# Seven products in place of eight for seven blocks, another cut of the tokens into blocks, and a written order of all operations

## The chip, the cores and the metric

One core of a Trainium2 chip runs the whole program. The metric is the device time of one execution in microseconds. TensorE (PE) multiplies, VectorE (DVE), ScalarE (ACT) and GpSimd (POOL) do the elementwise work, and SyncE (SP) issues most of the DMAs. Each engine runs its own instructions strictly in the order in which the program lists them, and waits at an instruction whose inputs are not there yet.

## The reference

Attention for 8 batches of 8 heads, 576 positions and 64 columns, twice (pooled by four, and in a band of seven positions), the sum of both, and then two dense layers:

```
q_d, k_d, v_d = mean of q, k, v over groups of 4 positions        # 144 groups
out_d     = softmax(q_d k_d^T / 8) v_d                            # repeated 4 times along the positions
out_local = softmax(q k^T / 8 where |i - j| < 4) v
x   = (out_up + out_local), as 4608 tokens x 512
h   = x @ w_in                                                    # 512 x 2048
out = (h - tanh(h)) @ w_out                                       # 2048 x 512
```

## The kernel before

**Attention.** Work goes by pairs of heads, p = 0 to 31, four pairs to a batch b. For each pair SP issues loads of k and q (`st`, two of 256 KB, `load_qk`) and of v in five overlapping tiles of 128 rows (`vst`, two of 160 KB, `load_v`). The 64 rows that are left of a batch's k and q come in two loads of their own (`sr`, `load_rest`). The casts to bf16 (`qr`, `vw`, `rr`) run on DVE, ACT or POOL. q and k are turned by PE for pairs 0 to 11 (`KIN`) and by a DMA for the others. PE makes the scores (`score1`, `score2`, matmuls with 64 contraction rows), ACT their exponentials (`E`), DVE multiplies by the band's mask, PE sums over v (`outs`, 18 matmuls), DVE divides (`ln`), and the result is turned back and added (`join`) into `xT`, a ring of three batches.

**Pooled v.** `vp` has 144 rows of group sums in two halves: groups 0 to 127, and groups 128 to 143 in the first 16 partitions of the second. For pairs 0 to 11 (`VIN`) PE makes it from `vw` with six matmuls against 0/1 matrices (`pool_v`, `pick`). For pairs 12 to 31 two loads bring v a third time (`load_v4`, 128 and 16 partitions, into buffers that were zeroed once), and two adds on POOL sum it (`pool_v4`, lines 440 and 444).

**Dense layers.** A block is a batch. The 576 columns of a batch in `xT` stand in the order (plane c, group g): column 144 c + g is position 4 g + c. A block kb takes the first 512 columns, and the last 64 of two batches share one more step (`left1`, `left2`). First layer: `mm1`, 16 steps of four 128x512 matmuls, then tanh on ACT (`u`, line 814) and the difference on DVE (`gT`, line 817). Second layer, blocks 0 to 4: `mm2`, 64 matmuls of 128x512 (line 883), four copies out of PSUM and 7 stores. Second layer, blocks 5 to 7 (`SEVEN`): a 2x2 cut of `gT` and `w_out` and seven products in place of eight, after Winograd. Each is 16 matmuls of 128x256 (`product`, line 1030). Its price elsewhere: `token_sums` (line 965) forms four sums of quarters of `gT`, in place for three of them; `weight_sums` (line 939) forms four differences of quarters of `w_out` once; and the results are added up through `keep0` and `y` (lines 1055 and 1101). The matmuls of the second layer of block kb - 1 are given to the planner among those of the first layer of block kb.

**Order.** Every operation is given to a `Plan` with an engine, a duration in ns, what it reads and writes, the PSUM banks that it may take and a priority (`pri`), sometimes an earliest time. `Plan.order` then puts them in order by playing them through on these durations, with a model of the DMA queue; where several engines could take an operation, a string `GIVEN` names the engine or leaves it open. Priority 5000 of the dense matmuls lets everything else go first. `emit` issues the instructions in this order; before the first matmul of block 1 it also puts matmuls on a zeroed tile into gaps (`filler`, line 1240). First-layer outputs and `mm2` outputs share PSUM banks 4 to 7 (`DENSE`), attention has banks 0 to 3.

**Start.** The first queue of w_in loads waits on POOL for the k load of pair 2 (`GATE`) and that of w_out for a v load (`OGATE`).

Of the kernel before, what the change touches and what calls it, by code (L numbers as in the profile page):

```python
# [14 lines left out]
class Plan:  # L15

    LAT = {"PE": 270, "ACT": 160, "DVE": 130, "POOL": 160, "SP": 50, "DMA": 1900,
           "DW": 1900}

    def __init__(self, given):
        self.ops = []
        self.given, self.choices = given, 0
        self.last_write = {}
        self.readers = {}
        self.users = {}  # L30
        self.place = {}

    def op(self, eng, ns, fn, reads=(), writes=(), pri=0, after=0.0, slack=0.0,
           port=False, opens=None, uses=(), choice=None, rows=128, share=0.4):
# [15 lines left out]
        names = set(uses)  # L50
        if opens and not isinstance(opens, list):
            opens = [opens]
        for o in opens or ():
            names.add(o[0])
        for n in names:
            self.users.setdefault(n, []).append(i)
        if choice:

            letter = self.given[self.choices]
            self.choices += 1  # L60
            named = [a[:4] for a in choice if a[0][0] == letter]
            choice = named or [a for a in choice if len(a) == 4]
        alts = {a[0]: a for a in choice} if choice else {eng: (eng, ns, fn, port)}
        self.ops.append(dict(alts=alts, deps=deps, pri=pri, after=after, slack=slack,
                             opens=opens, names=names, rows=rows, share=share,
                             what=(list(writes) + [None])[0]))
        return i

    def order(self):
        ops, n = self.ops, len(self.ops)  # L70
        users = [[] for _ in range(n)]
        left = [0] * n
        for i, o in enumerate(ops):
            left[i] = len(o["deps"])
            for d in o["deps"]:
                users[d].append(i)
        at = [o["after"] for o in ops]
        free, ready = dict.fromkeys(("PE", "ACT", "DVE", "POOL", "SP", "DMA"), 800.0), {}
        start, engine = [None] * n, [None] * n
        pending = {k: len(v) for k, v in self.users.items()}  # L80
        ends = {}
        bank_free = [0.0] * 8
        held = [None] * 8
        port_free = 0.0
        rows = 128
        self.held = []

        def make_ready(i):
            for eng in ops[i]["alts"]:
                ready.setdefault(eng, []).append(i)  # L90

        def seats(i):
            t, got, used = 0.0, [], set()
            for _, cs in ops[i]["opens"] or ():
                best = (float("inf"), None)
                for c in cs:
                    if any(held[b] is not None or b in used for b in c):
                        continue
                    best = min(best, (max(bank_free[b] for b in c), c), key=lambda x: x[0])
                if best[1] is None:  # L100
                    return float("inf"), None
                t = max(t, best[0])
                got.append(best[1])
                used.update(best[1])
            return t, got
        for i in range(n):
            if left[i] == 0:
                make_ready(i)
        for _ in range(n):
            best = None  # L110
            for eng, cand in ready.items():
                if not cand:
                    continue
                fr = free.get(eng, 0.0)
                if eng in ("DMA", "DW"):
                    i = min(cand, key=lambda i: (at[i], i))
                    now = max(fr, at[i])
                else:
                    now, i = None, None
                    eff = []  # L120
                    for c in cand:
                        t = max(at[c], seats(c)[0], fr)
                        if ops[c]["alts"][eng][3]:
                            t = max(t, port_free)
                        eff.append((t, c))
                    now = min(eff)[0]
                    if now == float("inf"):
                        continue
                    i = min((ops[c]["pri"], c) for t, c in eff if t <= now)[1]
                if best is None or now < best[0]:  # L130
                    best = (now, eng, i)
            if best is None:
                raise RuntimeError(f"no operation can be put next: {[(e, [(ops[c].get('what'), at[c], ops[c]['opens']) for c in cs[:6]]) for e, cs in ready.items()]} {held}")
            now, eng, i = best
            for other in ops[i]["alts"]:
                ready[other].remove(i)
            o = ops[i]
            _, ns, fn, port = o["alts"][eng]
            o["fn"], o["ns"] = fn, ns
            for (name, _), c in zip(o["opens"] or (), seats(i)[1] if o["opens"] else ()):  # L140
                self.place[name] = c
                for b in c:
                    held[b] = name
                self.held.append([name, c, now, None])
            start[i], engine[i] = now, eng
            if eng == "PE":

                if o["rows"] != rows:
                    ns += 60 if rows == 128 else 95
                rows = o["rows"]  # L150
            if eng == "DMA":

                ns *= 0.89 if now > 60000 else 0.82

                slow = max(0.0, free.get("DW", 0.0) - now)
                f = o["share"]
                ns = ns / f if ns <= f * slow else ns + (1 - f) * slow
            end = now + ns
            free[eng] = end
            if port:  # L160
                port_free = end
            for name in o["names"]:
                ends[name] = max(ends.get(name, 0.0), end + self.LAT[eng])
                pending[name] -= 1
                if pending[name] == 0:
                    for b in self.place[name]:
                        held[b] = None
                        bank_free[b] = ends[name]
                    for h in self.held:
                        if h[0] == name:  # L170
                            h[3] = ends[name]
            for u in users[i]:
                same = eng in ops[u]["alts"] and len(ops[u]["alts"]) == 1 and \
                    eng not in ("DMA", "DW")
                at[u] = max(at[u], end if same else end + self.LAT[eng] + ops[u]["slack"])
                left[u] -= 1
                if left[u] == 0:
                    make_ready(u)
        self.start, self.engine = start, engine
        return sorted(range(n), key=lambda i: (start[i], i))  # L180

    def emit(self, until=None, filler=None):
        order = self.order()
        stop = min([h[2] for h in self.held if h[0] == until], default=0.0)
        last = 600.0
        for i in order:
            o = self.ops[i]
            if filler and self.engine[i] == "PE" and self.start[i] <= stop:
                gap = self.start[i] - last
                if gap > 350:  # L190
                    busy = {b for _, c, s, e in self.held for b in c
                            if s < self.start[i] and e > last - 300}
                    rest = [b for b in range(7, -1, -1) if b not in busy]
                    if rest:
                        slow = 430 if self.start[i] < 6000 else 230
                        filler(rest[0], int(0.75 * gap / slow))
                last = self.start[i] + o["ns"]
            if o["fn"] is not None:
                o["fn"]()
# [3 lines left out]
def kernel(  # L203
# [48 lines left out]
           170.5, 170.5, 15, 153.5, 207.5, 209.5, 232.5, 235,  # L252
    ]

    GIVEN = (
        "..A..D.DADA.PADDADPDD.AADD..D.DD.AA.DA.ADAA....ADAD..AA..P...AP.D..AP....DDPPPDD"
        "..D..A.A...PAAAPPPAADDD.DDDDAD.ADAD.A..PPPDDDAA...A.....DA..A.AA.PD.D..ADPDDAP.P"
        "D.PP..D.DDDDD.P..DP...DADP...P....A...D.PP..DPAAPP..P.D..AD..A..DD.PPD.PA..D.P.."
# [213 lines left out]
    def attention(p):  # L472
# [248 lines left out]
        def outs():  # L721
            po = at(oname)
            for hh in range(2):
# [6 lines left out]
                for i in range(2):  # L730
                    to(1, EP + 256 * i + 128, vp[s][:, hh, i, :], False, i == 1)
# [540 lines left out]
```

## Time and profile before

| | us |
|---|---|
| median of three runs | 323.43 (322.58 to 326.46) |
| profiled execution, first to last instruction | 320.7 |
| DVE busy, all blocks | 255.3 |
| `L803` first layer, 512 matmuls, busy time | 124.6 |
| `L883` second layer of blocks 0 to 4, 320 matmuls | 78.6 |
| `L1030` seven products of blocks 5 to 7, in three groups by operand (144, 144, 48) | 18.3 + 17.8 + 6.1 |
| `L965` sums of quarters on DVE, blocks 5 to 7 | 6.4 + 4.3 + 4.2 |
| `L440`, `L444` adds of pooled v on POOL, 20 each | 25.4 and 14.6 |
| bytes moved by DMA | 59.23 MB |

A matmul's duration in the trace runs from its issue to a modelled end and overlaps the next one, so a group's mean (379 ns for 128x512) isn't what it costs in a row of matmuls. The cost is the distance from one start to the next, which the chain of waits gives: a piece of it is a stretch of one line's matmuls with start, length and count.

### The profile page before, as it was taken

What the parts mean: (1) busy time and instruction counts of PE and PEld (TensorE: products, weight loads), DVE (VectorE), ACT (ScalarE), POOL (GpSimd) and SP (SyncE); (2) the same over time, 40 slices, a digit from 0 to 9 for tenths busy, and PEclk for the clock granted to TensorE, in tenths of its full rate; (3) what the DMA queues carried; (4) which work ended last, traced back from release to release, by engine and by line L of the source; (5) the groups of instructions that cost most, each with busy time, mean ns of one, the idle gap of its engine ahead of it and who ended that gap; (6) DMA issues with size and microseconds to landing.
All of it is one profiled execution on the core that took longest, in us unless ns stands there. A gap on an engine that the chain in (4) does not pass through costs nothing.

```text
span 320.7 us, 7553 instructions
## 1 busy us (share of the span) xinstructions
PE 309.1 (96%) x2831; PEld 181.0 (56%) x2831; DVE 255.3 (80%) x451; ACT 207.8 (65%) x372; POOL 156.8 (49%) x185
## 2 busy tenths in 40 slices
PE   7978999999999999999999999999899999999994
PEld 3654546554754545454655444545476667666783
DVE  5685997597888898679888999899999797656853
ACT  5884995588856776369745878579766852455210
POOL 7822664326267473537464735357794653511000
PEclk9999999999999999999999999999999999999999
DMA  8999999999999999999999999995452143200414
GB/s 218 275 219 227 279 185 247 289 277 304 240 232 274 236 210 246 224 255 195 245 222 177 269 237 251 232 223 112 94 92 57 35 49 93 67 0 3 130 36 131
DMA packets 117205, 59.23 MB, mean 185 GB/s; under 512 B 85008, under 2 KB 112592, under 8 KB 117168
## 3 DMA queue, kind: packets, MB, share of 16 engines
q1 hardware_dynamic: 111584, 52.17, 71.3%
q0 software_dynamic: 4896, 5.97, 10.0%
q10 hardware_dynamic: 688, 0.61, 0.6%
q8 instruction: 22, 0.36, 0.4%
q14 instruction: 15, 0.12, 0.1%
HBM read 43.65 MB, written 9.44 MB: 166 GB/s over the span
## 4 chain that ended last, share of the span: by engine, by line
PE 88%; DMA 7%; DVE 1%; SPq 1%; ACT 0%; POOL 0%; ACTq 0%; issue 0%; POOLq 0%
PE ps L803 34%; PE ps L883 22%; PE ps L1030 11%; DMA vst<-in_v_dram 6%; PE ps L725 5%; PE ps L829 5%; PE ps L855 4%; PE ps L657 3%; DMA sr<-in_q_dram 1%; PE ps L671 1%; PE ps L510 1%; PE ps L458 1%; PE ps L767 1%; PE ps L665 1%; SPq L366 1%; DVE xT L760 1%
## 5 line engine op out<-in xcount | busy, mean ns | idle before, releaser
L803 PE MATMUL ps<-xT,w_in_sb 128*128 128x512 bf16 x512 | 124.6, 379 | 0.0
L817 DVE TENSOR_TENSOR gT<-ps,u 128x512 bf16<-128x512 f32 x128 | 86.0, 684 | 21.2 <-ACT u L814 19.6
L814 ACT ACTIVATE u<-ps 128x512 f32<-128x512 f32 x128 | 76.1, 599 | 36.2 <-PE ps L803 33.6
L883 PE MATMUL ps<-w_out_sb,gT 128*128 128x512 bf16 x320 | 78.6, 379 | 0.0
L803 PEld LDWEIGHTS <-w_in_sb 128*128 128x128 bf16 x512 | 47.1, 98 | 47.3 <-issue 0.4
L883 PEld LDWEIGHTS <-gT 128*128 128x128 bf16 x320 | 29.2, 98 | 31.2
L444 POOL TENSOR_TENSOR vp<-v 128x256 bf16<-128x256 f32 x20 | 14.6, 730 | 58.7 <-PE ps L725 48.1
L676 ACT ACTIVATE E<-ps 128x912 bf16<-128x912 f32 x32 | 29.8, 931 | 17.8 <-PE ps L665 14.6
L1030 PEld LDWEIGHTS <-gT 128*128 128x128 bf16 x288 | 27.9, 98 | 7.5
L742 DVE TENSOR_TENSOR ln<-ps,r 128x768 bf16<-128x768 f32 x32 | 30.6, 956 | 0.9
L711 DVE TENSOR_TENSOR E<-E,mask 128x1152 bf16<-128x1152 bf16 x29 | 25.6, 882 | 4.4 <-ACT E L680 4.2
L502 POOL CAST qr<-st 128x512 bf16<-128x512 f32 x32 | 22.5, 713 | 9.3 <-DMA st<-in_q_dram 6.0
L440 POOL TENSOR_TENSOR v<-v 128x512 f32<-128x512 f32 x20 | 25.4, 1271 | 1.1
L725 PEld LDWEIGHTS <-E 128*128 128x128 bf16 x576 | 21.7, 97 | 6.1
L684 ACT ACTIVATE E<-ps 128x576 bf16<-128x576 f32 x32 | 20.9, 654 | 0.0
L583 ACT COPY kt<-kq 128x576 bf16<-128x576 bf16 x16 | 18.9, 1180 | 2.9 <-DVE kq L578 2.7
L593 POOL TENSOR_TENSOR half<-kq 128x576 f32<-128x576 bf16 x13 | 18.1, 1389 | 3.6 <-DVE kq L578 1.5
L725 PE MATMUL ps<-vw,E 128*128 128x65 bf16 x320 | 18.9, 193 | 0.0
L760 DVE TENSOR_TENSOR xT<-lT 128x336 bf16<-128x336 bf16 (+1 forms) x30 | 18.4, 655 | 0.0
L1030 PE MATMUL ps<-Tw,gT 128*128 128x256 bf16 x144 | 18.3, 273 | 0.0
L725 PE MATMUL ps<-vp,E 128*128 128x65 bf16 x256 | 18.1, 193 | 0.0
L1030 PE MATMUL ps<-w_out_sb,gT 128*128 128x256 bf16 x144 | 17.8, 273 | 0.0
(118 smaller groups left out, 434.9 us busy)
## 6 DMA issues: line engine op xcount, KB each, us to landing
vst<-in_v_dram SPq DMA_DIRECT2D x64, 160.0 KB, 4.8
st<-in_k_dram SPq DMA_DIRECT2D x32, 256.0 KB, 4.6
st<-in_q_dram SPq DMA_DIRECT2D x32, 256.0 KB, 4.6
v<-in_v_dram SPq DMA_DIRECT2D x14, 256.0 KB, 3.6
w_in_sb<-in_moe_w_in_dram POOLq DMA_DIRECT2D x4, 512.0 KB, 12.7
w_out_sb<-in_moe_w_out_dram POOLq DMA_DIRECT2D x4, 512.0 KB, 12.2
out_dram<-y SPq DMA_DIRECT2D x7, 256.0 KB, 3.8
out_dram<-y SPq DMA_DIRECT2D x7, 224.0 KB, 3.1
```

What stands on the lines that cost most here:

```text
L440: eng.tensor_tensor(out=v2, in0=v4[s][:, :, :, 0:128], in1=v4[s][:, :, :, 128:256], op=ALU.add)
L502: (eng, ns, lambda dst=dst, src=src, fn=fn: fn(out=dst, in_=src), port)
L676: A.activation(out=E[s][:, :, E0:E0 + 456], in_=at(s1)[:, :, PS0:512], func=AF.Exp, scale=SCALE)
L711: eng.tensor_tensor(out=el, in0=el, in1=mask.unsqueeze(1).to_broadcast([128, 2, S]), op=ALU.mult)
L725: T.matmul(po[:, hh, 65 * n:65 * n + 65], E[s][:, hh, e:e + 128], vv, start=start, stop=stop)
L742: op("DVE", 960, lambda: V.tensor_tensor(out=ln[s].rearrange("p n (h d) -> p h n d", d=D), in0=blocks()[:, :, :, 0:64], in1=r[s].unsqueeze ...
L760: eng.tensor_tensor(out=dst, in0=src, in1=add, op=ALU.add)
L803: T.matmul(at(name)[:, 0, :], w_in_sb[:, dc, fc * 128:(fc + 1) * 128], xT[dc][:, c0:c0 + 512], start=(dc == 0), stop=(dc == N_DC - 1))
L814: op("ACT", 600, lambda: A.activation(out=u[us], in_=at(name)[:, 0, :], func=AF.Tanh), reads=[("hd", kb, fc)], writes=[("u", us)], pri=-1, ...
L817: op("DVE", 690, lambda: V.tensor_tensor(out=gT[g][:, fc, :], in0=at(name)[:, 0, :], in1=u[us], op=ALU.subtract), reads=[("hd", kb, fc), ( ...
L883: T.matmul(at(name)[:, 0, :], gT[g][:, fc, ts * 128:ts * 128 + 128], w_out_sb[:, fc, :], start=(fc == 0), stop=(fc == N_FF - 1))
L1030: T.matmul(dst, left[:, f, 128 * j:128 * j + 128], right[:, f, :], start=(first and e == 0 and f == 0 and (j == 0 or apart)), stop=(e == 1 ...
```

## The change

- `SEVEN` is `01111111`: blocks 1 to 4 also make seven products. `weight_sums` then comes with block 1; its earliest time of 180 us is gone.
- A block is made of groups 0 to 127 of all four planes: `mm1` reads `xT` as four runs of 128 columns. The last 16 groups of all planes, positions 512 to 575 of the batch, are the shared step. A pair of planes is then stored by one DMA (two runs of 2 KB per partition); 63 stores of `y` become 20.
- Pooled v: `vp` keeps groups 0 to 127 alone. The 16 groups that are left come for all 8 heads of a batch in one load (`load_vr`, 128 KB) and are summed and spread by three operations per batch on DVE or POOL (`pool_vr`) into `vpr`, which is zero outside a head's 16 partitions. `score2` takes the last groups' scores from a window that is shifted per head, so that they meet these partitions. `pool_v` has five matmuls, `load_v4` one DMA, and the adds of `pool_v4` are half as wide; they may go to DVE. The zeroing of `vp` and of the v4 buffers is gone.
- `Plan` no longer works out an order. Strings name it (`TURNS`), the engine of each choice (`ENGINES`), the banks (`BANKS`) and the filler matmuls (`FILL`, 22 of them; 19 before). The dependencies are checked; the durations in the calls are no longer used.
- The table of ACT's function is loaded by a copy of one element at the start.

```
-    SEVEN = [c == "1" for c in "00000111"]
+    SEVEN = [c == "1" for c in "01111111"]
...
-            for n, (i, t) in enumerate(((0, 0), (0, 1), (0, 2), (0, 3), (0, 4), (1, 4))):
-                T.matmul(pv[:, i, :], pick[:, n, :], vw[w][:, :, t, 0:D],
-                         start=n in (0, 5), stop=n in (4, 5))
+            for t in range(NT):
+                T.matmul(at(name)[:, 0, 0:2 * D], pick[:, t, :], vw[w][:, :, t, 0:D],
+                         start=t == 0, stop=t == NT - 1)
...
+    def load_vr(b):
+        base = v[b, 0]
+        load(500, lambda: nc.sync.dma_start(out=vr[b % 2], in_=bass.AP(
+            tensor=base.tensor, offset=base.offset + 512 * D,
+            ap=[[S * D, H], [4 * D, 16], [1, 4 * D]])),
+            [("vr", b % 2)], 520, 40 * b - 3000 + 4)
...
+        def spread(eng):
+            eng.tensor_tensor(out=vpr[b % 2], in0=vrp.unsqueeze(1).to_broadcast([128, H, D + 1]),
+                              in1=hsel.unsqueeze(2).to_broadcast([128, H, D + 1]), op=ALU.mult)
...
+        w0 = [128 - 16 * (2 * j + hh) for hh in range(2)]
...
-                             qkd[s][rows, 128 * i:128 * i + 128],
+                             qkd[s][rows, w0[hh] * i:w0[hh] * i + 128],
...
+                pools = vp[s][:, hh, :], vpr[b % 2][:, 2 * j + hh, :]
                 for i in range(2):
-                    to(1, EP + 256 * i + 128, vp[s][:, hh, i, :], False, i == 1)
+                    to(1, EP + 256 * i + 128, pools[i], False, i == 1)
...
-                         xT[dc][:, c0:c0 + 512], start=(dc == 0), stop=(dc == N_DC - 1))
+                         xT[dc][:, c0:c0 + S].rearrange("p (c g) -> p c g", c=4)[:, :, 0:128],
+                         start=(dc == 0), stop=(dc == N_DC - 1))
...
+            row = out[kb * S + 4 * r0 + 2 * half + js[0]]
+            (nc.sync if queue == "SP" else nc.scalar).dma_start(
+                out=bass.AP(tensor=row.tensor, offset=row.offset + lo,
+                            ap=[[4 * Dm, n], [Dm, len(js)], [1, hi - lo]]),
+                in_=y[ys][r0:r1, js[0]:js[-1] + 1, lo:hi])
...
+    def emit(self, filler):
+        turn = [self.number(self.turns[2 * i:2 * i + 2]) for i in range(n)]
...
+        for i in turn:
+            fn, deps, opens, names = self.ops[i]
+            assert deps <= done, "an operation stands before what it needs"
```

## The prediction

> **What bounds the kernel now.** First the head of the page and its slices.
>
> ```profile
> span 320.7 us, 7553 instructions
> PE 309.1 (96%) x2831; PEld 181.0 (56%) x2831; DVE 255.3 (80%) x451; ACT 207.8 (65%) x372; POOL 156.8 (49%) x185
> PE   7978999999999999999999999999899999999994
> DVE  5685997597888898679888999899999797656853
> PEclk9999999999999999999999999999999999999999
> DMA  8999999999999999999999999995452143200414
> PE 88%; DMA 7%; DVE 1%; SPq 1%; ACT 0%; POOL 0%; ACTq 0%; issue 0%; POOLq 0%
> ```
>
> PE is full from the fourth slice to the last but one at an undisturbed clock, and it is 88% of the chain of waits (last line); DMA's 7% lies in the first 30 us. DMA, too, is full, but only until slice 27 (some 216 us). Since "busy" PE can hide slow matmuls, I read the chain's pieces (start, us, what) for the cost of one matmul and for the idle moments.
>
> ```profile
> 29.60 0.73 POOL vw L427
> 30.38 0.51 PE ps L458 x6
> 62.50 0.45 PE ps L458 x6
> 127.24 5.61 PE ps L883 x26
> 144.65 5.18 PE ps L803 x24
> 230.18 1.08 DVE E L711
> 295.02 1.79 PE ps L829 x32
> 304.24 12.24 PE ps L1030 x112
> ```
>
> 128x512 costs 0.216 us (5.61/26, 5.18/24), a product's 128x256 costs 0.109 (12.24/112), a step of the shared tokens 0.056 (1.79/32), a `pick` matmul 0.075 at most (0.45/6). From 30.38, where the wait for `vw` of pair 4 ends, PE waits once: about 1.1 us around 231, behind the mask multiply on DVE. It ends at 304.24 + 12.24 = 316.48; last add and store take the other 4.2.
>
> All matmuls of the program at these prices (attention's by the starts in the trace) are 291.1 us, 14.9 of them before 30.38. So 276.2 us of matmuls take 286.1. Of the 9.9 left over 1.1 is the wait, and 8.1 lies where PE goes from full matmuls to score matmuls of 64 rows and back: by the starts in the trace 0.096 on the way in, 0.12 on the way out, 0.02 between the groups, 37 times. Nothing else is lost: what PE no longer does, the kernel no longer takes, as long as the others keep up.
>
> **The products.** In blocks 1 to 4, 256 matmuls at 0.216 (55.3 us) become 448 at 0.109 (48.8): -6.5 us, all on the path. The rows that bear on a risk of it are the weight loads:
>
> ```profile
> L829 PEld LDWEIGHTS <-w_in_sb 128*128 128x128 bf16 x256 | 15.1, 98 | 3.2 <-issue 1.3
> L1030 PEld LDWEIGHTS <-gT 128*128 128x128 bf16 x288 | 27.9, 98 | 7.5
> ```
>
> 98 ns for a weight load of the full array. The change adds 192 loads; exposed, they would cost 18.8 us. The rows exclude it: a step of 0.056 with a load of 0.098 for each matmul is only possible if loads overlap matmuls, and 0.109 would be 0.207. The Trainium skill (TensorE: Matmul & The Clock Gate, the section on packing small matmuls) says that a weight load overlaps running matmuls only when its row group differs; all these loads take the whole array, so by it this change would lose. The trace disagrees, so it stays a rival with a small chance.
>
> **Pooled v.** Twelve pairs with five `pick` matmuls for six: 12 x 0.06 to 0.075, -0.8 us. Operand runs of 128 columns in `mm1` and of 16 in the shared step: no row shows the latter; `L657` reads runs of 28 in 215 ns a matmul, as `L665` does runs of 30 in 216, so I take nothing, with +14 us (a doubled 0.056 for 256 steps) as the far end, held unlikely by these rows.
>
> **Order on PE.** By the program's listing, score groups are entered 31 times after the first dense run, not 37: 6 x 0.22, -1.2 us with the few steps between groups. The wait at 231 is not in a written order by itself: -1.1, or 0 if it returns.
>
> **The start.** PE can run dense once batch 0's `xT` and the first w_in chunk are there. Before:
>
> ```profile
> 13.33 3.17 POOL L408 DMA_DIRECT2D w_in_sb<-in_moe_w_in_dram  x4
> 14.33 1.03 SPq L390 DMA_DIRECT2D vst<-in_v_dram  x2
> 20.54 6.72 SPq L390 DMA_DIRECT2D vst<-in_v_dram  x2
> ```
>
> The four w_in DMAs land at 22.3, 25.7, 29.0 and 33.1 by the trace's landings, and while they run SP's own loads crawl: `vst` of pair 4, issued at 14.85, lands at 29.45, and PE waits for it until 30.38. In the new listing POOL issues the first two w_in chunks only behind both casts of pair 4, whose q is the 19th load on SP. SP's first 16 loads land 0.84 us apart from 3.70 on, and three of the 19 are half loads: about 18.2. A cast of 0.7, issue at 18.9; the first chunk then lands 8.9 later as before, 27.8, the second 3.4 after it. The v of pairs 0 to 3 comes before that (about 20.5 for the last, pair 2's), and cast, pick, sums, division, turn and join follow in some 5 us, so `xT` is there first. On PE two matmuls and a score group lead; the long run starts at 28.5 with 13.9 us of work behind it, where before it was 30.38 with 14.9: -0.9. Ends: -3.5, if the chunk comes at 25, limited by `xT`; +4, if it takes the 12.7 us that the page gives as w_in's median. The third and fourth chunk follow eight and four POOL operations later and land by this reckoning at 35 to 41, a few us ahead of their matmuls; w_out, if issued at 40 (38.2 before), lands from 47 to 60 by the spacing of before (4.2), and the listing takes block 0's second layer quarter by quarter of w_out between 49 and 59: tight, a us late at the end.
>
> **Cover by the other engines.** DVE, by each operation's mean: sums of quarters 5.4 us and adds 2.1 per block, four blocks, so +30; the weight differences (8 x 0.78) only move forward. The strings take away copies of `y`, `kt` and `keep` (9.8), joins (9.2), pooled sums of q and k (7.4), casts and others (5): by the rows -1, and with 29 new small operations, whose nearest row is a copy of 256 columns (`L463`, 0.42; I take 0.3), +8 of 277. POOL: 40 us of `L440` and `L444` shrink to about 15, joins, `qkd` and casts come in. ACT +3 to 7. None is on the path if DVE holds.
>
> ```profile
> 30.00:300.00 270.00, 268.65 (x2382) 152.53 (x2382) 224.57 (x373) 185.06 (x328) 139.98 (x156) 1.00 0.83 186
> 180.00:220.00 40.00, 40.00 (x320) 19.72 (x319) 37.16 (x63) 29.48 (x50) 19.86 (x23) 1.00 0.97 228
> ```
>
> (us, PE, PEld, DVE, ACT, POOL, clock, DMA.) DVE is at 83% between 30 and 300 and was held at 93% for 40 us with PE full. Its 225 us become about 233 in 260: 90%. The DMA's transfers come to the same sum (`vr` +1 MB, the 16-partition loads -0.6, fewer stores); batch 3's last input lands at 99 before, and block 3 now starts some 13 us earlier, at about 126: cover remains.
>
> New waits have no row. I take +1.5 us (the last w_out chunk, or one wait like that at 231), from 0 to 7, one of 1 us for each of seven blocks.
>
> **Sum.** -6.5 - 0.8 - 1.2 - 1.1 - 0.9 + 1.5 = -9.0: span 311.7. The median lies 2.7 above this span, so 323.4 - 9.0 = 314.4.
>
> **Rivals.** (a) *The gain is mostly given back in waits*: start +4 in place of -0.9, new waits 7 in place of 1.5: 314.4 + 10.4 = 324.8; half of that, 319.6, is its likely form. For: the start's chunks are just in time. Against: one wait of 1.1 us in 286 shows how well these streams can be packed. Chance 0.22, within 2%. (b) *DVE takes over in blocks 1 to 4, slower*: sums of quarters read all of a block's `gT` in place, so a late DVE holds `gT`, the four banks that `mm1` writes into fill, and PE stands. It decides where DVE, as the pacer, is busy for less than 83%: 233/0.83 = 281 us between start and tail in place of 260, +18 to 20, time 333. Behind a late sum there wait `gT` (128 x 0.684), and ACT's tanh for its buffers.
>
> ```profile
> DVE gT L817 <- ACT u L814: 19.6, 39, 2.7
> ```
>
> This idle time of DVE is of that sort, it waits for ACT. Against: 93% between 180 and 220. Chance 0.05. (c) *Weight loads exposed*, at every product of blocks 1 to 4: -9.0 + 18.8, time 333; it decides from the first product on. Chance 0.03. This is what the rule of the Trainium skill named above would do here. (d) *More is gained*: start -3.5, no new waits: 310.3. Same verdict as the forecast. That seven products are made at all is settled by the listing: 784 matmuls on the line of the products, 64 on that of `mm2`.
>
> **Numbers.** Forecast with (d) 0.70, (a) 0.22, (b) and (c) 0.08. The range goes from (d), 310, to the middle of (a), 320.5, which leaves some 0.1 above and less below. Two per cent, 317.0 and 329.9, is about what runs between 322.6 and 326.5 can tell from no change. A forecast from 310 to 317 is faster by over 2%; (a) lies within; (b) and (c) are slower.
>
> **What would show it.** Right: in the chain pieces of the products' line at 0.109 a matmul in blocks 1 to 4; a last matmul near 307.5; `L803`'s successor starting its long run at 27 to 30; PE's waits together under 3 us after it. Wrong: a chain with DVE or `gT` in it for some us per block (b); product steps above 0.15 (c); the shared step above 0.056; PE waiting for w_in or w_out between 28 and 58 (a).

## The result and the profile after

The changed kernel takes 371.9 us (median of four runs, 371.1 to 376.9) where the kernel before takes 324.1 (one run more than in the table above): the ratio, taken without the slowest run of the changed kernel, is 1.146 with a 95% interval of 1.139 to 1.152. The forecast was 314.4 us and the range ended at 320.5. The profiled execution has a span of 369.4 us instead of 320.7.

The head of the page of after, its row of granted clock and its chain by line:

```profile
span 369.4 us, 7865 instructions
...
PE 355.5 (96%) x3014; PEld 219.7 (59%) x3014; DVE 265.5 (72%) x463; ACT 211.0 (57%) x380; POOL 173.8 (47%) x221
...
PEclk9999999999699999999589999998589999996599
...
PE ps L782 26%; PE ps L1003 20%; PE ps L809 15%; PE ps L835 5%; DMA vst<-in_v_dram 4%; PE ps L863 4%; PE ps L705 3%; DMA w_in_sb<-in_moe_w_in_dram 3%; DVE gT L938 2%; DMA st<-in_q_dram 2%; PE ps L635 2%; DMA sr<-in_k_dram 1%; DVE gT L797 1%; DVE S L938 1%; PE ps L651 1%
```

PE is as full as before, 96%, so the engines do not starve it: it is busy for 46 us longer (355.5 against 309.1). The third biggest line of the chain is L809, the first layer of the shared step (`left1`, L829 before), 15% of 369 us. And the granted clock, 9 in every slice before, falls to 5 or 6 in four places. Pieces of the chain (start, us, what) give the price of a step:

```profile
84.38 3.56 PE ps L809 x16
88.98 7.14 PE ps L809 x32
...
118.86 2.59 PE ps L782 x12
...
155.34 1.75 PE ps L1003 x16
...
353.27 11.80 PE ps L1003 x108
```

A step of the shared tokens costs 0.223 us (3.56/16, 7.14/32), four times the 0.056 of before. A product in block 2 (155) and in block 7 (353) costs 0.109, `mm1` 0.216, as forecast. The group of L809 shows it as well, once one knows that its mean of 400 ns per matmul contains the overlap with the next:

```profile
L809 PE MATMUL ps<-xT,w_in_sb 128*128 128x128 bf16 x256 | 58.3, 400 | 0.0
L809 PEld LDWEIGHTS <-w_in_sb 128*128 128x128 bf16 x256 | 30.3, 118 | 26.9 <-issue 0.6
```

58.3 us of busy time for 256 matmuls, with an idle time of 0.0 before them: nothing is waited for, the matmul itself is slow. In the windows below (us, then busy time and count of PE, PEld, DVE, ACT, POOL, the granted clock, DMA share, GB/s) the second and fourth hold passes of the shared step:

```profile
110.00:168.00 58.00, 56.95 (x565) 38.42 (x564) 55.89 (x87) 44.69 (x77) 39.53 (x44) 1.00 1.02 225
168.00:192.00 24.00, 24.00 (x126) 13.06 (x125) 13.42 (x23) 7.98 (x14) 6.23 (x11) 0.72 0.63 129
192.00:248.00 56.00, 54.94 (x498) 35.98 (x497) 46.64 (x73) 40.39 (x69) 33.65 (x37) 1.00 0.88 192
...
328.00:352.00 24.00, 24.00 (x98) 11.77 (x97) 11.25 (x16) 6.54 (x12) 0.00 (x0) 0.64 0.06 23
```

Until the last matmul the clock falls only where the shared step runs, to 0.72 and 0.64 on average in these windows. By the trace's records it is at 0.5 for 6.83, 13.65, 13.65 and 17.07 us, beginning 3.4 to 8.2 us after the pass does. The first time is at 92.43, so the sixteen steps from 84.38 on took their 0.223 us while the clock was still at 1.00: the clock isn't what makes the step slow.

I added up all distances between the starts of neighbouring matmuls from 31 us to the last one, and split them by the prices above. `runs16_keep` is an experiment further down, the changed kernel with two repairs. Full price is what each matmul costs in an undisturbed row.

| from 31 us on, against before | forecast | after | `runs16_keep` |
|---|---|---|---|
| all matmuls at full price (275.5 before) | -7.3 | -6.5 | -6.7 |
| changes to and from score matmuls (8.1) | -1.2 | -1.1 | -0.8 |
| waits of PE (1.3) | +0.4 | +5.1 | +7.5 |
| shared step above 0.056 (0.2) | 0 | +42.6 | -0.1 |
| other matmuls while the clock is at 0.5 | 0 | +8.4 | 0 |
| sum | -8.1 | +48.5 | -0.1 |

The forecast's ninth microsecond, -0.9 for an earlier start, lies before 31 us. PE had done 19.4 us of matmuls by then in after and 19.5 before, but that counts the filler matmuls, which compute nothing: 22 of 0.216 us in after, 18 before. Without them it is 14.6 against 15.6, so the start came out about 0.9 us worse instead of better. The same 0.9 explains the first row: over the whole program the matmuls other than fillers fall by some 7.4 us, as forecast, but more of them lie behind 31 us.

### The profile page after: what moved, and what is told of

Its sections match the earlier page's. It is cut to its first block, busy times and chain, and to the rows that moved or that the text cites. A ratio compares the mean times of both kernels' runs of the same rounds, so it can differ in the third digit from the quotient of the medians.

```text
span 369.4 us, 7865 instructions
## 1 busy us (share of the span) xinstructions
PE 355.5 (96%) x3014; PEld 219.7 (59%) x3014; DVE 265.5 (72%) x463; ACT 211.0 (57%) x380; POOL 173.8 (47%) x221
## 4 chain that ended last, share of the span: by engine, by line
PE 78%; DMA 10%; DVE 8%; issue 2%; ACT 1%; ACTq 0%; SPq 0%; POOL 0%; DVEq 0%; POOLq 0%
PE ps L782 26%; PE ps L1003 20%; PE ps L809 15%; PE ps L835 5%; DMA vst<-in_v_dram 4%; PE ps L863 4%; PE ps L705 3%; DMA w_in_sb<-in_moe_w_in_dram 3%; DVE gT L938 2%; DMA st<-in_q_dram 2%; PE ps L635 2%; DMA sr<-in_k_dram 1%; DVE gT L797 1%; DVE S L938 1%; PE ps L651 1%
## 5 line engine op out<-in xcount | busy, mean ns | idle before, releaser
L794 ACT ACTIVATE u<-ps 128x512 f32<-128x512 f32 x128 | 73.6, 599 | 38.6 <-PE ps L782 35.0
L1003 PEld LDWEIGHTS <-gT 128*128 128x128 bf16 x672 | 65.6, 100 | 20.5 <-issue 3.4
L782 PEld LDWEIGHTS <-w_in_sb 128*128 128x128 bf16 x512 | 48.0, 98 | 48.5 <-issue 1.4
L809 PE MATMUL ps<-xT,w_in_sb 128*128 128x128 bf16 x256 | 58.3, 400 | 0.0
L809 PEld LDWEIGHTS <-w_in_sb 128*128 128x128 bf16 x256 | 30.3, 118 | 26.9 <-issue 0.6
L1003 PE MATMUL ps<-w_out_sb,gT 128*128 128x256 bf16 x336 | 45.9, 283 | 0.5 <-DVE y L1027 0.5
L577 POOL TENSOR_TENSOR qkd<-half 128x288 bf16<-128x288 f32 x25 | 23.9, 957 | 45.2 <-DVE half L572 28.0
L1003 PE MATMUL ps<-Tw,gT 128*128 128x256 bf16 x336 | 42.3, 273 | 2.7 <-DVE gT L938 1.5
L822 DVE TENSOR_TENSOR gL<-ps,u 128x512 bf16<-128x512 f32 x16 | 11.1, 691 | 41.8 <-ACT u L820 41.8
L484 POOL CAST qr<-st 128x512 bf16<-128x512 f32 x40 | 27.1, 685 | 29.4 <-DMA kq<-qr 14.6
L820 ACT ACTIVATE u<-ps 128x512 f32<-128x512 f32 x16 | 9.6, 597 | 46.8 <-PE ps L809 46.8
L1074 POOL TENSOR_TENSOR y<-y,keep 128x512 f32<-128x512 f32 x12 | 17.0, 1414 | 16.2 <-ACT y L1024 16.2
L1024 ACT COPY y<-ps 128x512 f32<-128x512 f32 x19 | 11.1, 586 | 21.0 <-PE ps L1003 19.2
```

The costliest lines, as they stand in the source:

```text
L484: (eng, ns, lambda dst=dst, src=src, fn=fn: fn(out=dst, in_=src), port)
L577: eng.tensor_tensor(out=pooled, in0=half[:, 0:288].rearrange("p (n x) -> p n x", n=2), in1=half[:, 288:576].rearrange("p (n x) -> p n x", ...
L782: T.matmul(at(name)[:, 0, :], w_in_sb[:, dc, fc * 128:(fc + 1) * 128], xT[dc][:, c0:c0 + S].rearrange("p (c g) -> p c g", c=4)[:, :, 0:128 ...
L794: op("ACT", 600, lambda: A.activation(out=u[us], in_=at(name)[:, 0, :], func=AF.Tanh), reads=[("hd", kb, fc)], writes=[("u", us)], uses=[n ...
L809: T.matmul(at(name)[:, 0, 128 * f:128 * f + 128], w_in_sb[:, dc, (f0 + f) * 128:(f0 + f) * 128 + 128], xT[dc].rearrange("p (b c g) -> p b ...
L1003: T.matmul(dst, left[:, f, 128 * j:128 * j + 128], right[:, f, :], start=(first and e == 0 and f == 0 and (j == 0 or apart)), stop=(e == 1 ...
```

## The experiments

**Why the shared step is slow.** The line of the diff that I misread is the operand's last one:

```
xT[dc].rearrange("p (b c g) -> p b g c", b=NR, c=4)[:, s0:s0 + 2, 128:G]
```

`p b g c` lets the plane c run fastest. Columns that follow each other are 144 columns (288 bytes) apart, and the 16 neighbours of a plane are never read one after the other. `runs16` only turns the two dimensions, and the rows of the store with them:

```
-  xT[dc].rearrange("p (b c g) -> p b g c", b=NR, c=4)[:, s0:s0 + 2, 128:G]
+  xT[dc].rearrange("p (b c g) -> p b c g", b=NR, c=4)[:, s0:s0 + 2, :, 128:G]
...
-  ap=[[Dm, LEFT], [1, Dm]]
+  ap=[[Dm, 4], [4 * Dm, LEFT // 4], [1, Dm]]
```

> The changed kernel, but the shared step takes its 128 columns plane by plane (runs of 16 neighbouring columns) in place of group by group (every column 144 columns from the last), and its rows are stored to the same places. Theory (single-column steps): the 256 matmuls of the shared step fall from 0.223 us to 0.056, -42.7 us, the clock stays at 1.00 and the some 6 us of half-clock matmuls go too: 317 to 324 us. Rival (short runs or many dimensions of the operand): 0.223 stays, and so does 372 us. Rival (clock first): a slow clock makes the step slow; then at most a factor of 2 is in it and the clock still falls.

Measured: 328.9 us, 1.014 times the kernel before (1.007 to 1.020). The same group in `runs16`:

```profile
L809 PE MATMUL ps<-xT,w_in_sb 128*128 128x128 bf16 x256 | 15.4, 219 | 0.0
```

15.4 us for 58.3, a step is back at 0.056, and the clock no longer falls in these places. The time falls by 43 us, by the order in which one operand is read; short runs or many dimensions as such cost nothing. The time is still 5 us above the expected range, which is taken up below. The reverse is `before_strided`: the kernel before, with nothing of the change but such an order of columns in its shared step, which so computes the first layer of other tokens.

```
-  xT[dc].rearrange("p (b c) -> p b c", c=S)[:, s0:s0 + 2, 512:S]
+  xT[dc].rearrange("p (b x g) -> p b g x", b=NR, g=G)[:, s0:s0 + 2, 128:G]
```

> The kernel before, with one read changed: the shared step reads its 64 + 64 columns in the order that takes single columns 144 apart (it computes other columns, in another order). Theory (single-column steps): 0.223 us for each of 256 matmuls, +42.7 us, the clock falls to 0.5 some 8 us after each of the four steps begins, +4 to 8 us: 371 to 375 us. Rival (the written order loses time by itself): this kernel stays below the changed kernel's 372 by what the order loses.

Measured: 379.8 us, 1.171 times before (1.164 to 1.178). Its group and a window with a pass of the shared step:

```profile
L829 PE MATMUL ps<-xT,w_in_sb 128*128 128x128 bf16 x256 | 59.5, 400 | 1.0 <-DVE gT L817 1.0
```
```profile
338.00:362.00 24.00, 23.78 (x105) 13.05 (x105) 7.94 (x12) 2.98 (x5) 0.00 (x0) 0.64 0.14 44
```

One access pattern is enough for the loss, and for the clock: 0.64 in this window, at 0.5 for 61 us altogether. Both kernels carry 42.7 us of slow steps; what this one has beyond that, some 15 us, is other work at half clock and waits, more than the 4 to 8 us expected for it.

**Which distance costs.** Three single runs of the kernel before with other columns in the four passes (m) of its shared step. `scan` takes every second column, then runs of 2, 8 and 16 columns with as many left out:

```
+  if m == 0: x[:, :, 448:576], every second column
+  run, k = ((2, 4), (8, 16), (16, 32))[m - 1]
```

> The kernel before, with the shared step of each pair of blocks reading its 128 columns in another pattern (other columns are computed): every second column; runs of 2 with a step of 4; runs of 8 with a step of 16; runs of 16 with a step of 32. Theory (a step other than one column is what costs): 0.223, then three times 0.056. Rival (the cost goes by the bytes of a run): 0.223 or more, then 0.11, then 0.056 twice, or a slow fall over all four.

The pieces of its chain, one for each pass:

```profile
87.89 1.95 PE ps L837 x32
...
158.27 0.92 PE ps L837 x16
...
235.87 2.23 PE ps L837 x40
...
297.82 1.79 PE ps L837 x32
```

All four near 0.056 to 0.061 (1.95/32, 0.92/16, 2.23/40, 1.79/32). That any step but one column costs is refuted: leaving out every second column costs next to nothing (a median of 0.058). `scan2` reads the same 64 columns of a batch in transposed order, so that neighbours are 4, 8, 16 and 32 columns apart:

```
+  k = (4, 8, 16, 32)[m]
+  ...[:, s0:s0 + 2, 512:S].rearrange("p b (n k) -> p b k n", k=k)
```

> The kernel before, in which the shared step reads its 64 columns per batch in another order: single columns that lie 4, 8, 16 and 32 columns apart (8, 16, 32 and 64 bytes) in the four passes m = 0 to 3. The shared step's results are those of the same tokens in another order, so the output has them in the wrong rows. Theory: a matmul costs more as soon as each column lies in another piece of 16 bytes: 0.056 us a step at 4 columns, about 0.22 at 8 (as the selection matmul of before, 60 ns for 32 columns, 8 columns apart), 16 and 32. Rival: the price grows with the distance, 0.056 to 0.08 at 8 columns and 0.22 only near 144. In the passes where it is 0.22 the granted clock falls to 0.5 for some us, some 4 to 8 us after the pass begins, and stays at 1.0 in the others.

Its pieces by pass, and the clock's row of its page:

```profile
88.85 3.83 PE ps L834 x32
...
162.04 3.57 PE ps L834 x16
...
255.94 8.93 PE ps L834 x40
...
328.76 3.94 PE ps L834 x32
```
```profile
PEclk9999999999999999998689999999858999999999
```

The steps are 0.117 (median of the pass) at 8 bytes, 0.223 at 16 and at 32 bytes, 0.123 at 64. My theory had 0.056 for the first and 0.22 for the last and was wrong at both ends; growth with the distance is refuted too. The clock falls in the two passes at 0.223 (slices 19 to 21 and 29 to 31 of 9 us each) and in neither of the others. The last pass was not a clean case: 64 columns with a step of 32 leave only two far columns before the next pair. `scan3` takes that apart: single columns 6 bytes apart; 16 bytes apart and only going forward; four columns 64 bytes apart; two columns 288 bytes apart.

```
+  m == 0: every third column of 192
+  m == 1: every eighth column of 512
+  n, k, w = ((4, 32, 16), (2, 144, 32))[m - 2]
+  x[:, :, 0:n * k].rearrange("p b (n k) -> p b k n", k=k)[:, :, 0:w]
```

> The kernel before, in which the shared step reads other columns, so that its results are those of other tokens: single columns 3 apart (6 bytes) in pass m = 0, single columns 8 apart that only go forward (64 per batch) in m = 1, four columns that lie 32 apart, then the next four, in m = 2, and two columns that lie 144 apart, then the next two, in m = 3. Theory (a piece of 16 bytes is read in 1.74 ns, and used for as many columns as lie in it one after the other): 0.084 us at 3 columns (2.7 columns a piece), 0.223 in m = 1, 2 and 3. Rival, by the 0.123 that two columns 32 apart took: two pieces can be kept at hand, so that m = 3 takes 0.12, while four far pieces (m = 2) take 0.223. By distance alone m = 0 would take 0.056 to 0.08 and m = 3 0.223.

Its pieces by pass:

```profile
88.66 2.91 PE ps L838 x32
...
160.48 3.65 PE ps L838 x16
...
254.34 8.69 PE ps L838 x40
...
326.61 3.94 PE ps L838 x32
```

Medians 0.088, 0.228, 0.217 and 0.123. This fits a read in pieces of 16 bytes at 1.74 ns each (0.223/128): eight adjacent columns, or four with every second left out, share a piece and hide it behind their own 0.44 ns a column (0.056/128); every third column, 2.7 to a piece, would give 0.084, two to a piece 0.111, one to a piece 0.223 (measured 0.088, 0.117 and 0.217 to 0.228). The Trainium skill (Advanced Engine Details and Errata, SBUF Cachelines) names lines of 16 bytes and a penalty for another line at each access, which agrees. It asks for at least two hits on a line to absorb the latency; here two were not enough: two columns in a line took 0.117, twice the full-speed step, and only four took 0.058. What two alternating far columns do, 0.123 at 64 and at 288 bytes, follows from neither: the theory had 0.223 for the last pass of `scan3`. The rival, that two pieces are kept at hand, had the number, but only because it was taken from `scan2`; by the prices above, two kept pieces would be read while their sixteen columns pass, and the step would be 0.056. Why it is 0.123 stays open.

**What is left without the slow step.** `runs16` loses 1.4% where the forecast, without this step, has a gain of 2.8%. Its waits on PE (us in total, times, longest) and the copy that heads the list, on ACT:

```profile
PE ps L1003 <- ACT keep L1024: 4.6, 3, 2.1
PE ps L1003 <- DVE gT L938: 2.1, 2, 1.3
PE ps L651 <- POOL qkd L577: 1.6, 1, 1.6
PE ps L1003 <- DVE gT L797: 1.1, 1, 1.1
PE ps L782 <- DMA w_in_sb<-in_moe_w_in_dram: 0.8, 1, 0.8
```
```profile
179.20 0.58 ACT L1024 COPY keep<-ps 128x512 f32<-128x512 f32 x1 [3.30 <-DMA out_dram<-keep]
```

Product 1's result goes to `keep0`. The shared step stores its own result from `keep0` just before, and the copy waits 3.30 us until these stores have landed. PE stands behind it, since the next product needs the bank. `runs16_keep` gives the shared step a tile of its own (`vrs`, a scratch row of the pooled v, is held in bf16 to make room):

```
+  keepL = fixed("keepL", [128, 512], FP32)
-  ("ACT", 590, lambda: A.copy(out=keep0, in_=at(name)[:, 0, :]), False),
+  ("ACT", 590, lambda: A.copy(out=keepL, in_=at(name)[:, 0, :]), False),
... (the copy on DVE and the two stores likewise)
-  vrs = fixed("vrs", [128, 2 * D], FP32)
+  vrs = fixed("vrs", [128, 2 * D], BF16)
```

> The changed kernel with the shared step read plane by plane, and besides with a result tile of its own for the shared step's second layer (`left2`), so that the copy of the next block's first product no longer waits until the two stores out of `keep0` have landed (to make room a scratch row of the pooled v, `vrs`, is held in bf16). Order of all operations as before. Theory: the three waits of PE at 179.8 (2.27 us), 249.3 (1.81) and 316.7 (1.05) behind these copies vanish, 5.1 us, and nothing else is late at those places, so 328.9 becomes about 324, level with the kernel before (ratio 0.995 to 1.005). Rival: the waits are elastic, because DVE (228 of 270 us busy between 30 and 300) is next behind: PE then stands for `gT` or its sums some microseconds later, and less than 2 us are gained (ratio 1.008 to 1.014).

Measured: 322.9 us, ratio 0.998 (0.995 to 1.001): level with the kernel before, and 6 us below `runs16`. The waits on `keep` are gone and none of their size takes their place:

```profile
PE ps L1004 <- DVE gT L939: 1.5, 2, 0.8
PE ps L1004 <- DVE gT L798: 1.2, 1, 1.2
PE ps L706 <- DVE E L692: 0.9, 2, 0.6
PE ps L783 <- DVE xT L742: 0.6, 2, 0.3
PE ps L1004 <- DVE y L1028: 0.5, 1, 0.5
```

By the sum over all starts 8.8 us of waits are left, against 1.3 before: they eat the 7.5 us that matmuls and changes give. Nearly all name DVE. Is DVE too busy? `nomask_after` takes work off it: the band's mask goes onto 64 of 576 columns only, in the kernel of `runs16_keep`; `nomask_before` has the same cut in the kernel before.

```
-  eng.tensor_tensor(out=el, in0=el, in1=mask.unsqueeze(1).to_broadcast([128, 2, S]), op=ALU.mult)
+  eng.tensor_tensor(out=el[:, :, 0:64], in0=el[:, :, 0:64],
+                    in1=mask[:, 0:64].unsqueeze(1).to_broadcast([128, 2, 64]), op=ALU.mult)
```

> The changed kernel with the shared step read plane by plane and with a result tile of its own for the shared step, in which the band's mask is multiplied onto the first 64 of 576 columns only (27 multiplies on DVE of 0.74 us, 5 on POOL, become short): the rest of the mask is left out. All else and the order stay. Theory: the waits that are left on PE (8.8 us after 31, against 1.3 in the kernel before) are DVE's, whose sums of quarters stand behind other work; with some 17 us taken off DVE they fall to 2 to 3 us, and the time from 322.9 to 316 to 318. Rival: they are latency in the written order (results, sums and copies that follow one another too closely, whatever else DVE does): the waits stay above 6 us, and the time above 320.

> The kernel before with the same part of the mask left out. It has one wait, 1.1 us at 231, which is for a masked E. Theory (what limits it is PE's matmuls alone): only that wait goes, 322.4 from 323.5, so that the difference to the changed kernel with the same cut is 5 us or more, the part of the forecast's gain that came out of matmul prices and changes between score and other matmuls. Rival: DVE also limited the kernel before, and it gains as much as the other: the difference stays under 2 us.

Measured: 0.998 times before for the first (0.993 to 1.002), 0.998 for the second (0.996 to 1.001). Neither gains, and the difference of 5 us between them did not come, nor did the gain of both that the rival of `nomask_before` had. The waits of `nomask_after`:

```profile
PE ps L1004 <- DVE gT L939: 1.5, 2, 0.8
PE ps L1004 <- DVE gT L798: 1.0, 1, 1.0
PE ps L1004 <- DVE y L1028: 0.9, 1, 0.9
PE ps L652 <- POOL qkd L578: 0.9, 1, 0.9
```

The wait for sums of quarters is the same to a tenth, 1.5 in two places, and all waits add up to 7.9 us. DVE's busy time between 30 and 300 us fell from 232.8 to 218.8, so the waits do not follow DVE's load as a whole. But the cut gave DVE no free time where the longest wait is, the one for `gT` that ends at 137.86 in `runs16_keep` and at 137.10 in `nomask_after` (windows of `runs16_keep`, then of `nomask_after`; the third number of busy time is DVE's):

```profile
126.00:139.00 13.00, 11.85 (x103) 7.74 (x102) 12.83 (x17) 11.45 (x21) 9.65 (x11) 1.00 1.16 275
126.00:139.00 13.00, 11.94 (x104) 7.81 (x102) 12.83 (x17) 10.71 (x19) 9.32 (x11) 1.00 1.13 294
```

DVE is busy for 12.83 of 13 us there in both. For this wait the run decides nothing. `relief` does more: it moves 24 operations of the pooled v, expected to be 14 us, from DVE to POOL in the strings:

```
-  "DDDPPDAPPAAPPDPPDAPPDAPPDPDDAPDAAPDDPDPPPDPAAPPDPDDDDDDDPDDAPPAADPDPDDAPPAAPPDPDDAPPAAPP"
+  "DDDPPPAPPAAPPDPPPAPPDAPPDPPPAPDAAPDDPPPPPDPAAPPDPPPDDDDDPPPAPPAADPDPPPAPPAAPPDPPPAPPAAPP"
...
```

> The changed kernel with the shared step read plane by plane and a result tile of its own for the shared step, in which 24 operations of the pooled v (`pool_vr` and `pool_v4`, from batch 3 on) go to POOL and none to DVE. DVE loses some 14 us, POOL (162 of 270 us busy between 30 and 300) gains some 20. Theory: the waits for sums on DVE shrink by 2 to 4 us, and 322.9 becomes 319 to 321, ratio 0.985 to 0.993. Rival: POOL's own casts, joins and sums come later behind the longer operations, and PE waits for `xT` or E instead: 323 or more.

Measured: ratio 1.001 (0.997 to 1.005), the rival's result, and the waits come to 9.5 us:

```profile
PE ps L1004 <- DVE gT L939: 2.8, 3, 1.3
PE ps L783 <- DVE xT L742: 1.7, 2, 0.9
PE ps L652 <- POOL qkd L578: 1.3, 1, 1.3
PE ps L783 <- POOL xT L742: 1.0, 1, 1.0
```

The total is no better, but the waits are others. The longest wait of `runs16_keep` is gone (the same product in `runs16_keep`, then in `relief`):

```profile
137.86 1.36 PE L1004 MATMUL ps<-Tw,gT 128*128 128x256 bf16 x11 [1.15 <-DVE gT L798]
136.06 1.47 PE L1004 MATMUL ps<-Tw,gT 128*128 128x256 bf16 x12
```

Ahead of it 2.5 us of pooled v left DVE, which speaks for a busy DVE as the cause there. Two others, of 0.9 us each by the starts, at 200 and 269, are nearly the same in all three runs; between the last `gT` and these products DVE does nothing but sums of quarters and, at 269, one add of `y`. This is latency in the written order: the product stands so soon after the last `gT` that PE arrives first, whatever else DVE does. And new or longer waits take the place of the one that went, for POOL's `qkd` at 101, for `xT` at 130, 247 and 248, and for a sum of quarters at 169. DVE was relieved by less than planned: between 30 and 300 us its busy time fell by 6.6 us (232.8 to 226.1) while POOL's rose by 19 (161.9 to 181.1). Some of DVE's other operations took longer; one sum of quarters took 2.51 us at 166 in `relief` and 1.21 at 167 in `runs16_keep`. Why was not tried, and neither was another order.

**Seven products alone.** `seven_only` is the kernel before with its planner, all blocks 1 to 7 with seven products, and nothing else of the change:

```
-  SEVEN = [c == "1" for c in "00000111"]
+  SEVEN = [c == "1" for c in "01111111"]
...
-  writes=[("T", n, e)], pri=4000, after=180000.0, port=True)
+  writes=[("T", n, e)], pri=4000, after=60000.0, port=True)
```

> The kernel before with seven products in blocks 1 to 4 too, under the old planner, with all their sums on DVE, and nothing else. If PE alone decides: 448 matmuls at 0.109 for 256 at 0.216, -6.5 us, 317 us. If DVE needs relief elsewhere, as the rival of the prediction had it (30 us more on DVE between 60 and 220, where it was 85 to 93% busy): waits of PE for DVE of 10 us and more, 328 to 340 us.

A single run takes 346.0 us, above the 328 to 340 of its worse case. Its window from 100 to 140 us, and the longest of its waits:

```profile
100.00:140.00 40.00, 29.65 (x289) 17.59 (x290) 34.84 (x55) 25.57 (x43) 25.72 (x25) 0.96 0.89 187
```
```profile
PE ps L803 <- DVE gT L817: 7.7, 9, 2.4
PE ps L1030 <- DVE y L1055: 2.8, 1, 2.8
PE ps L1030 <- DVE Tw L939: 2.2, 2, 1.7
```

PE works 29.65 of 40 us here and waits for `gT`: without the rest of the change the products cost more than they save. Against `runs16_keep`, what comes with the products in the change (the written order, the pooled v, the cut of the blocks) is worth some 23 us.

## Why the prediction was wrong

**The step that failed** is in the paragraph on pooled v: "Operand runs of 128 columns in `mm1` and of 16 in the shared step: no row shows the latter [...] so I take nothing, with +14 us [...] as the far end, held unlikely by these rows". Three things in it were wrong. The shared step has no runs of 16; the plane runs fastest, and each column lies 288 bytes from the one before, or, at the change to the next group, 862 bytes back. The rows put forward, `L657` and `L665`, read runs of 28 and 30 and say nothing about single columns; their 215 and 216 ns are besides mean durations, which contain the overlap and are no cost. And the far end was a doubled step, where a fourfold one was measured: 256 x (0.223 - 0.056) = 42.7 us. The kernel before did have a row for it, the selection matmul of L622, which reads 32 columns, each eight columns (16 bytes) from the last, and whose starts are mostly 60 ns apart: 1.9 ns a column, beside 0.46 for L725, 65 adjacent columns in 30 ns. As an estimate by that row the shared step comes to 0.24 (128 x 1.9 ns) and the forecast to 361 (314.4 + 256 x 0.184). The expectation that the step would show itself "above 0.056" was the right sign to look for.

**The clock** was no term of the sum. At half clock the other matmuls cost 8.4 us more than at full. It is a consequence of the same line: it falls with the steps of 0.217 to 0.228 in `after`, in `before_strided` and in both scans that have them, and in the four changed kernels without them it stays at 1.00 from 31 us to the last matmul.

**The waits**, "+1.5 us, from 0 to 7", in place of the 1.1 us at 231, measured +5.1 net in after and +7.5 in `runs16_keep`, which is rival (a)'s price of a microsecond per block. In part they are latency of the order, in part DVE's load (see `relief`); how they divide is open. In `runs16` the store that holds `keep0` comes on top. I had looked at the copies and stores as work and not at which tile they share.

**The start**, -0.9, came out at about +0.9: the long run of `mm1` begins at 30.25 in after and 31.7 in `runs16`, not at 28.5, with 14.6 us of work done by 31 us instead of 15.6.

**What held.** Products at 0.109 in all seven blocks, so some -7.4 for all matmuls of the program (forecast with the five `pick` matmuls: -7.3), -6.5 of it behind 31 us; -1.1 for the changes to and from score matmuls (forecast -1.2). Weight loads stayed hidden, rival (c): 0.109 a step with loads of 98 to 100 ns. DVE did not take over, rival (b), though `seven_only` shows that it does without the other parts. With the read and the shared tile mended, the change is worth nothing rather than 9 us. That is rival (a) with its waits in full (8.8 us for 7), but not with its +4 at the start.

## What to carry to other kernels

Write out the order in which a matmul's moving operand visits its columns, innermost dimension first, before pricing it; if neighbours leave a 16-byte piece at each step, the matmul took four times as long here (twice, where only two far columns alternated), and the cure is a swap of two dimensions with the matching swap where the result is stored. Such a matmul shows no wait: PE is 100% busy, and only the distance between starts and the mean of its group (400 ns for 219) betray it. And when work is taken from an engine that is full, ask for each result tile who still reads it, a store in flight included.

## What the runs showed of the hardware

- A moving operand of single bf16 columns costs 0.44 to 0.45 ns a column at steps of 2 and 4 bytes, 0.69 at 6, 0.91 at 8, 1.7 to 1.8 from 16 bytes on (0.056, 0.058, 0.088, 0.117, 0.217 to 0.228 us for 128 columns). Two far columns in turn take about half of that, 0.123 for 128; why is open.
- The granted clock falls to 0.5 while PE is busy without a gap (24.00 of 24.00 us from 168 to 192), in stretches of 1 to 5 times 3.41 us. It did so in every pass at 0.22 us a step and in none at 0.12 or below. The Trainium skill (TensorE: Matmul & The Clock Gate, on HAM oscillation) warns of idle gaps above some 3.4 us. No gap of this kind is in these passes; a PE that is fed at a quarter of its rate seems to be enough. In `seven_only`, whose shared step is at 0.056, the clock fell too, for 3.41 us from 130.4 and again from 144.0, where PE waits much (busy for 29.65 of 40 us from 100 to 140); from 100 us to there no two starts are further apart than 2.75 us.
